# Matmuls that add zero, put into TensorE's stream after each tile's scores and PV

## The chip, the cores and the metric

One core of a Trainium2 chip (trn2). The metric is the device time of one execution in microseconds (us). Before the change: 1116.29 us, the median of 3 runs (1116.23 to 1120.81).

## The reference

Two attention blocks over 2048 tokens with 32 heads of 16 columns; their outputs stand side by side.

```python
def _B_ref(x, wqkv, wo):                       # problem "b": plain attention
    qkv = (x @ wqkv) ...                       # q, k, v: 32 heads x 2048 x 16
    scores = jnp.einsum('bhqd,bhkd->bhqk', q, k) * Dh ** (-0.5)
    o = jnp.einsum('bhqk,bhkd->bhqd', _softmax(scores), v)
    return o... @ wo
def _A_ref(x, wq, wk, wv, wo, beta):           # problem "a": 4 segments of 512 tokens
    for s in range(N):                         # causal attention inside the segment
        a_dot = _softmax(qs @ ks * scale + mask) @ vs
        a_mem = (phi(qs) @ M) / (phi(qs) @ z + 1e-06)     # memory of earlier segments
        o = g * a_mem + (1.0 - g) * a_dot
        M = M + phi(ks).T @ vs;  z = z + phi(ks).sum()
    ...
```

## The kernel before

Everything hangs on the exponentials of the scores. The kernel deals the scores out in 848 tiles, of 3 and 2 banks in turn (1536 and 1024 columns; a bank stands for 512 columns in PSUM here). For each tile TensorE (PE) computes up to three 32-row score matmuls at once (in the timelines below three take 0.61 us together at half clock), ScalarE (ACT) takes the exponential into `pT`, and two tiles later TensorE multiplies it with V (PV) into the accumulator `acc`. Some scores go to VectorE (DVE) instead, through `v_ps` and `vx`. Projections and other small work ("chores") are put between the tiles.

```python
BANKS = (3, 2); LAG = 2; VSHARE = 0.95
...
mp = ps_a = ms.enter_context(tc.tile_pool(name="ps_a", bufs=3, space=PSUM))  # acc, v_ps and chores
...
def scores(t):
    pt = last_s[0] = ps_s.tile([P, BANKS[t % 2], 512], F32, name="s_ps", tag=f"s{t % 2}")
    ...                                       # 32-row matmuls, one to a bank
    pin(nc.scalar.activation(pT[:, 0:n, :], pt[:, 0:n, :], ACT.Exp, scale=SCALE))
...
for t in range(NT):                           # program order of every engine
    now[0] = t
    run_until(t)                              # chores that are due
    scores(t)
    did = pv(t - LAG, 2)                      # up to two groups of 4 PV matmuls
    ...
    for _ in range((0 if did else 1) + ...):
        step_chore()                          # a matmul or so of a chore
    vfill((0.08 + 0.427 * len(tiles[t][0])) * VSHARE - ...)   # VectorE's pieces
```

The score tiles have two buffers. TensorE can write tile t+1 only when ScalarE has finished tile t-1 (its score matmuls wait 134.9 us for that in before), and should be done before ScalarE finishes tile t.

Of the kernel before, what the change touches and what calls it, by code (L numbers as in the profile page):

```python
# [13 lines left out]
BF16 = mybir.dt.bfloat16  # L14
# [5 lines left out]
P = 128  # L20
# [5 lines left out]
W = 512  # L26
# [8 lines left out]
XSCALE = SCALE * 1.4426950408889634 * 1024  # L35

C0, C1, C3 = 0.4580543, 0.4656991, 0.0762947
VSHARE = 0.95
VQUADS = 2
BANKS = (3, 2)  # L40
# [5 lines left out]
def kernel(  # L46
# [13 lines left out]
    nc = tc.nc  # L60
# [7 lines left out]
    def pin(ins):  # L68
        return tc.keep_in_program_order(ins)

    def mm(*a, **k):
        return pin(nc.tensor.matmul(*a, **k))  # L72
# [42 lines left out]
    def masks_gates():  # L115
        pin(nc.gpsimd.memset(bd[:], 0.0))
        for j in range(4):
            q = slice(32 * j, 32 * j + 32)
            for e in range(2):
                pin(nc.gpsimd.tensor_scalar(bd[q, e, q], bd[q, e, q], par[q, e:e + 1], None, ALU.add))  # L120
        pin(nc.scalar.activation(gcol[:], beta_t[:], ACT.Exp, scale=-1.0))
        pin(nc.vector.tensor_scalar(gcol[:], gcol[:], 1.0, None, ALU.add))
        pin(nc.vector.reciprocal(gcol[:], gcol[:]))
        pin(nc.vector.tensor_scalar(omg[:], gcol[:], -1.0, 1.0, ALU.mult, ALU.add))
        gv = gcol[:].rearrange("p (rt e) -> p rt e", e=2)
        pin(nc.vector.tensor_scalar(grow[:], gv[:, :, 0], par[:, 0:1], None, ALU.mult))
        pin(nc.vector.scalar_tensor_tensor(grow[:], gv[:, :, 1], par[:, 1:2], grow[:], ALU.mult, ALU.add))
# [192 lines left out]
    with ExitStack() as ms:  # L320
        big = ms.enter_context(tc.tile_pool(name="big", bufs=1))
        wk = ms.enter_context(tc.tile_pool(name="wk", bufs=1))
# [37 lines left out]
        for name, ch, rt in order:  # L360
            us = [dict(name=name, ch=ch, rt=rt, e=e, id=len(units) + e) for e in range(2)]
# [29 lines left out]
        first_tile, tiles = {}, []  # L391
# [102 lines left out]
        def bq_chores(ch, rt):  # L494
            qB[ch, rt] = wk.tile([P, 2, W], BF16, name="qB", tag=f"qB{rt}")
            key = ("b", ch, rt)
            chore(min(first_tile[key], first_tile.get(("v", ch, rt), NT)), do_q(mp, wk, wB, xTB[ch], rt, qB[ch, rt]))
# [16 lines left out]
        def flush():  # L514
            todo, held[0] = held[0], []
            for us, f in todo:
                credit[0] -= us
                f()

        current, now = [None], [0]  # L520

        def step_chore(new=True):

            flush()
            if current[0] is None:
                i = next((i for i, c in enumerate(chores) if c[4] <= now[0]), None)
                if not new or i is None:
                    return False
                current[0] = chores.pop(i)
            try:  # L530
                next(current[0][2])
                current[0][3] = max(1, current[0][3] - 1)
            except StopIteration:
                current[0] = None
                return step_chore(new)
            return True

        def run_until(t):
            while (current[0] is not None and current[0][0] <= t) or (chores and chores[0][0] <= t):
                step_chore()  # L540
# [6 lines left out]
        for rt in range(NRT):  # L547
            bq_chores(0, rt)
        okm = wk.tile([P, 2], F32, name="okm")
        last_s, cur = [None], [0]  # L550
        pvq = []
        accs, OT = {}, {}
# [45 lines left out]
        def vpiece(wq):  # L598

            w = wq[0]  # L600
            credit[0] -= w[1]
            w[1:] = next(w[0], None), True
            if w[1] is None:
                wq.popleft()
# [4 lines left out]
        def vfill(us):  # L609
            credit[0] = min(credit[0] + us, 1.4)  # L610
            while vfin or vwork:
                wq = vfin or vwork
                if wq is vwork and live[0] == 3 and not wq[0][2]:
                    return
                if credit[0] - sum(us for us, _ in held[0]) < 0.5 * wq[0][1]:
                    return
                vpiece(wq)
# [49 lines left out]
        def unit_done(u):  # L667
            name, ch, rt, e = u["name"], u["ch"], u["rt"], u["e"]
            st = fin[(name, ch, rt)]
            if e == 0:  # L670
                vdrain(vfin)
            fin_unit(wk, st, accs.pop(u["id"])[:], e)
            if u["id"] >= 62:
                flush()
                fin_half(wk, st, e)
                if e == 0:
                    sums_ok(wk, 0, 63, okm[:, 0:1])
                return
            if e == 0:
                return  # L680
            if (name, ch) not in OT:
                OT[(name, ch)] = wk.tile([P, NRT, W], BF16, name=f"OT_{name}", tag="OT", bufs=3)
            ot = OT[(name, ch)]
            while name == "a" and ch and ("mem", ch, rt) not in seen:
                step_chore()
            flush()

            def finish():
                yield from fin_pair(wk, st, name, rt, u["id"] - 1, ot[:, rt, :])
                i = order.index((name, ch, rt))  # L690
                if rt == NRT - 1:
                    due = first_tile[order[i + 1]] + 50 if i + 1 < len(order) else 10 ** 6
                    for sb in range(4):
                        chore(due, do_out(mp, wk, name, ot, woA if name == "a" else woB, ch, sb), 5)
            vpush(vfin, finish())
            if name == "a" and ch < NSEG - 1:
                mem_chores(ch, rt)
                seg_chores(ch + 1, rt)
            if name == "b" and ch < NSEG - 1:
                bq_chores(ch + 1, rt)  # L700

        def pv(t, lim):

            if cur[0] == len(units):
                return False
            u = units[cur[0]]
            ready = [q for q in pvq if q["u"] is u and q["t"] <= t and len(q["parts"]) == 4]
            if not ready or (lim == 2 and len(ready) < 2 and quads_left[u["id"]] > len(ready)):
                return False
            for q in ready[0:lim]:  # L710
                pvq.remove(q)
                live[0] -= "v" in q
                if u["id"] not in accs:
                    accs[u["id"]] = ps_a.tile([P, W], F32, name="acc", tag="misc")
                first = ("acc", u["id"]) not in seen
                seen.add(("acc", u["id"]))
                quads_left[u["id"]] -= 1
                v = vA[u["ch"]] if u["name"] == "a" else VB
                for pT, sl, j, (_, kb, col, w, c0) in q["parts"]:
                    h = 8 * u["rt"] + 2 * j + u["e"]  # L720
                    mm(accs[u["id"]][32 * j:32 * j + 32, c0:c0 + w], v[:, kb, VW * h:VW * h + 32],
                       pT[:, sl, col:col + w], start=first, stop=(quads_left[u["id"]] == 0),
                       tile_position=(0, 32 * j), skip_group_check=True)
            if quads_left[u["id"]] == 0:
                cur[0] += 1
                unit_done(u)
            return True

        for t in range(NT):
            now[0] = t  # L730
            run_until(t)
            scores(t)
            if t == 6:
                masks_gates()
            did = pv(t - LAG, 2)

            rate, n = 0.0, current[0][3] if current[0] else 0
            for c in chores:
                n += c[3]
                rate = max(rate, n / max(1, c[0] - t))  # L740
            for _ in range((0 if did else 1) + (rate > 0.55) + (rate > 1.1) + (rate > 1.8)):
                step_chore()
            vfill((0.08 + 0.427 * len(tiles[t][0])) * VSHARE - (0.69 if tiles[t][1] else 0.0))
            flush()
        vdrain(vfin)
# [15 lines left out]
        while len(pvq) > 1:  # L761
            assert pv(NT, 1)
        last = ps_s.tile([P, BANKS[NT % 2], 512], F32, name="l_ps", tag=f"s{NT % 2}")
        partial(0, last[:, 0, :])
        assert pv(NT, 1)
        partial(1, last[:, 1, :])
        tN = fin[("b", NSEG - 1, NRT - 1)]["tN"]
        for sb in range(4):
# [3 lines left out]
               skip_group_check=True)  # L772
# [157 lines left out]
```

## Time and profile before

| | before |
|---|---|
| time, median | 1116.29 us |
| ScalarE busy | 1005.5 us, 90% |
| TensorE mean granted clock | 0.632 |
| first to last exponential (trace) | 1084.7 us |
| floor of the 848 exponentials (trace) | 424 x (1331 + 904) ns = 948 us |

The granted clock is the share of full rate at which TensorE was let run; the clock records show only 1.0 and 0.5, and the mean stands in the table. Each stretch at one clock, but for the last, lasts a whole number of steps of 3.41 us (in before 1 to 45 of them). The floor is worked out from the 10th percentile of start-to-start times: 1331 ns after a 1536-column tile and 904 ns after a 1024-column one, counted from the trace. What the tiles take over it is called "lost" below: about 137 us.

From the page of before: busy time by engine, then busy tenths in 40 slices of the span, and the granted clock in tenths.

```profile
span 1118.5 us, 15007 instructions
...
PE 903.0 (81%) x5690; PEld 197.8 (18%) x5753; DVE 798.7 (71%) x1143; ACT 1005.5 (90%) x877; POOL 216.4 (19%) x361
...
PE   6898888797888787887898798787777887777775
...
ACT  3799999897889989999899879999999999999994
...
PEclk9989955555558866566555757555565576555556
```

ScalarE is nearly full; TensorE has half its clock in most slices after the fifth.

The groups of ScalarE by shape (busy us, mean ns of one, idle before it, what ended most of that idle time):

```profile
L635 ACT ACTIVATE pT<-s_ps 128x1536 bf16<-128x1536 f32 x424 | 619.2, 1460 | 70.7 <-PE s_ps L72 57.3 <-PE v_ps L72 7.8 <-ACT pT L635 0.6
L635 ACT ACTIVATE pT<-s_ps 128x1024 bf16<-128x1024 f32 x424 | 437.7, 1032 | 23.8 <-PE v_ps L72 11.6 <-PE s_ps L72 7.5 <-POOL pT L654 1.4
```

Idle before exponentials: 70.7 + 23.8 = 94.5 us.

Three stretches of before. The columns are the stretch, its length, busy us and number of instructions of PE, PEld, DVE, ACT and POOL, then the granted clock, the DMA share and GB/s:

```profile
40.00:150.00 110.00, 94.44 (x718) 26.75 (x722) 80.51 (x128) 103.51 (x92) 39.72 (x73) 0.93 0.04 10
150.00:700.00 550.00, 456.83 (x2808) 99.80 (x2842) 410.90 (x590) 494.88 (x433) 123.57 (x181) 0.60 0.03 9
700.00:1080.00 380.00, 304.01 (x1915) 59.22 (x1923) 280.17 (x379) 368.60 (x319) 33.73 (x58) 0.56 0.01 4
```

### The profile page before, as it was taken

The page shows a single profiled execution, that of the slowest core. Times are in us where ns is not written, and L with a number is a line of the kernel's source. Part 1 is how long each engine was busy: PE and PEld are TensorE (multiplying, and loading weights), DVE is VectorE, ACT ScalarE, POOL GpSimd, SP SyncE. Part 2 cuts the span into 40 slices and gives each one's busy share as a digit, 9 for nine tenths or more (in the row PEclk, how much of TensorE's full clock was granted, in tenths as well). Part 3 has the DMA queues.
Part 4 walks back from the last instruction along what each step waited for, and adds up shares of the span by engine and source line. Part 5 has one row for each costly group of instructions (what it writes and reads, how often), then busy time and mean ns, then how long its engine had stood idle before and what let it go on. Part 6 is the DMA issues. An engine that isn't in the chain of part 4 may idle for free.

```text
span 1118.5 us, 15007 instructions
## 1 busy us (share of the span) xinstructions
PE 903.0 (81%) x5690; PEld 197.8 (18%) x5753; DVE 798.7 (71%) x1143; ACT 1005.5 (90%) x877; POOL 216.4 (19%) x361
## 2 busy tenths in 40 slices
PE   6898888797888787887898798787777887777775
PEld 1222211111112211121111112111111121111111
DVE  2667877774778877779776867878577777876752
ACT  3799999897889989999899879999999999999994
POOL 3722310403213022141402304212020300000000
PEclk9989955555558866566555757555565576555556
DMA  7300000001000000000000000000000000000000
GB/s 183 81 6 20 6 1 5 1 1 23 6 1 4 31 11 5 1 20 10 1 4 2 19 20 6 6 1 1 1 1 1 1 29 10 1 1 1 1 1 23
DMA packets 34578, 15.23 MB, mean 14 GB/s; under 512 B 26304, under 2 KB 34496, under 8 KB 34496
## 3 DMA queue, kind: packets, MB, share of 16 engines
q1 hardware_dynamic: 32768, 12.47, 4.7%
q10 hardware_dynamic: 1728, 1.70, 0.5%
q8 instruction: 47, 0.77, 0.3%
q14 instruction: 35, 0.29, 0.1%
HBM read 4.20 MB, written 4.19 MB: 8 GB/s over the span
## 4 chain that ended last, share of the span: by engine, by line
ACT 39%; PE 33%; issue 12%; DVE 9%; POOL 5%; DMA 1%; SPq 0%; ACTq 0%; DVEq 0%; POOLq 0%
ACT pT L635 38%; PE s_ps L72 13%; PE acc L72 9%; PE v_ps L72 3%; DVE vv L572 3%; POOL pT L654 3%; PE k_ps L72 2%; PE q_ps L72 2%; PE o_ps L72 2%; DVE vv L569 1%; DVE vx L643 1%; ACT ex L182 1%; POOL qA L174 1%; DMA xT_a<-in_A_x_dram 1%; POOL po L184 1%
## 5 line engine op out<-in xcount | busy, mean ns | idle before, releaser
L635 ACT ACTIVATE pT<-s_ps 128x1536 bf16<-128x1536 f32 x848 | 993.2, 1246 | 94.5 <-PE s_ps L72 64.8
L72 PE MATMUL s_ps<-qB,KB 32*128 32x512 bf16 x1800 | 408.5, 555 | 136.3 <-ACT pT L635 123.2
L643 DVE TENSOR_SCALAR vx<-v_ps 128x512 uint16<-128x512 f32 x248 | 169.7, 684 | 124.0 <-PE v_ps L72 120.4
L72 PE MATMUL acc<-pT,VB 128*32 128x512 bf16 x1800 | 223.3, 576 | 5.2 <-DVE vx L643 4.8
L72 PEld LDWEIGHTS <-KB 32*128 32x128 bf16 x2048 | 86.6, 98 | 509.4 <-issue 506.1
L654 POOL TENSOR_SCALAR_AFFINE_SELECT pT<-pT 128x256 bf16<-128x256 bf16 (+2 forms) x242 | 108.7, 478 | 317.2 <-ACT pT L635 316.4
L72 PE MATMUL v_ps<-qB,KB 32*128 32x512 bf16 x248 | 137.1, 553 | 7.0 <-DVE aT L250 3.9
L243 DVE STREAM_TRANSPOSE tT<-acc 128x512 f32<-128x512 f32 x64 | 45.6, 712 | 66.0 <-PE acc L72 65.5
L569 DVE TENSOR_SCALAR vv<-vv 128x2048 f16<-128x2048 f16 x124 | 86.6, 698 | 2.0
L572 DVE TENSOR_TENSOR vv<-vx 128x2048 f16<-128x2048 f16 x62 | 77.5, 1250 | 1.3
L72 PE MATMUL s_ps<-qA,kA 32*128 32x384 bf16 (+3 forms) x512 | 66.0, 364 | 15.4 <-ACT pT L635 11.7
L572 DVE TENSOR_TENSOR vv<-vv,vi 128x2048 uint16<-128x2048 uint16 x62 | 76.2, 1230 | 1.3
L572 DVE TENSOR_TENSOR vv<-vv,vx 128x2048 f16<-128x2048 f16 x62 | 76.1, 1228 | 1.3
L174 POOL TENSOR_SCALAR qB<-qc,par 128x512 bf16<-128x512 bf16 x32 | 32.9, 1038 | 203.8 <-DVE qc L171 203.8
L72 PEld LDWEIGHTS <-VB 128*32 128x32 bf16 x2048 | 36.0, 105 | 117.5 <-issue 117.4
L174 POOL TENSOR_SCALAR qA<-qc,par 128x512 bf16<-128x512 bf16 x32 | 25.7, 815 | 127.8 <-DVE qc L171 127.7
L72 PE MATMUL acc<-pT,vA 128*32 128x128 bf16 (+3 forms) x512 | 43.5, 371 | 6.6 <-POOL pT L654 6.1
L569 DVE TENSOR_SCALAR vx<-vx 128x2048 uint16<-128x2048 uint16 x62 | 44.7, 721 | 1.5
L569 DVE TENSOR_SCALAR vi<-vx 128x2048 uint16<-128x2048 uint16 x62 | 43.1, 695 | 1.0
L72 PE MATMUL acc<-vv,VB 128*32 128x512 bf16 x248 | 36.8, 582 | 2.9 <-DVE vv L572 2.4
L171 DVE CAST qc<-q_ps 128x512 bf16<-128x512 f32 x32 | 22.0, 687 | 19.8 <-PE q_ps L72 15.2
L72 PE MATMUL k_ps<-xT_a,w_a 128*128 128x512 bf16 x58 | 26.6, 499 | 10.2 <-DMA xT_a<-in_A_x_dram 9.5
(151 smaller groups left out, 536.6 us busy)
## 6 DMA issues: line engine op xcount, KB each, us to landing
out_dram<-osb SPq DMA_DIRECT2D x31, 128.0 KB, 1.7
w_b<-in_B_wqkv_dram SPq DMA_DIRECT2D x3, 512.0 KB, 4.9
phk<-phkT SPq DMA_TRANSPOSE x48, 2.3
w_a<-in_A_wk_dram ACTq DMA_DIRECT2D x1, 512.0 KB, 4.1
w_a<-in_A_wq_dram ACTq DMA_DIRECT2D x1, 512.0 KB, 5.8
w_a<-in_A_wv_dram ACTq DMA_DIRECT2D x1, 512.0 KB, 8.1
wo_a<-in_A_wo_dram SPq DMA_DIRECT2D x1, 512.0 KB, 4.5
wo_b<-in_B_wo_dram SPq DMA_DIRECT2D x1, 512.0 KB, 5.4
```

The source lines that it names most:

```text
L72: return pin(nc.tensor.matmul(*a, **k))
L171: vlater(0.69, lambda: pin(nc.vector.tensor_copy(qc[:], ps[:])))
L174: pin(nc.gpsimd.tensor_scalar(dst[:, e, :], qc[:], par[:, e:e + 1], 0.0, ALU.mult, ALU.add))
L182: pin(nc.scalar.activation(ex[:], src, ACT.Exp))
L184: pin(nc.gpsimd.tensor_scalar(po[:], src, 0.0, None, ALU.max))
L243: vlater(0.72, lambda: pin(nc.vector.transpose(st["tT"][:, e].rearrange("p c d -> p (c d)"), acc)))
L569: pin(nc.vector.tensor_scalar(o, i, s1, s2, op0, op1))
L572: pin(nc.vector.tensor_tensor(o, i0, i1, op=op))
L635: pin(nc.scalar.activation(pT[:, 0:n, :], pt[:, 0:n, :], ACT.Exp, scale=SCALE))
L643: pin(nc.vector.tensor_scalar(x[0][:, vb[0], :], vt[:], XSCALE, 32768.0, ALU.mult, ALU.add))
L654: pin(nc.gpsimd.affine_select(out=blk, in_=blk, compare_op=ALU.is_ge, fill=0.0, base=0, pattern=[[0, len(sls)], [1, P]], channel_multiplie ...
```

## The change

The intent: TensorE's granted clock seems to follow its activity (counted in the trace of before, it fell after steps in which something streamed for 0.42 of the time or less, and rose after steps with 0.70 or more), so give it activity. The change keeps an account of TensorE's work per tile, in us at full clock. Where it falls behind 0.72 of the time of ScalarE's tile, 128x128 matmuls with zero weights and zero data are put into the stream. They add zero to the accumulator that is open, so they need no PSUM buffer of their own and alter no result.

```diff
+PESHARE = 0.72
...
+        work = [0.0]
...
                 next(current[0][2])                    # a step of a chore
+                work[0] += 0.17
...
+        zeros = wk.tile([P, W], BF16, name="zeros")
+        nc.gpsimd.memset(zeros[:], 0.0)
+        def idle_work(us):
+            work[0] = max(work[0] - us * PESHARE, -1.0)
+            acc = accs.get(cur[0])
+            while acc is not None and work[0] < -0.11:
+                mm(acc[:], zeros[:, 0:P], zeros[:], start=False, stop=False, skip_group_check=True)
+                work[0] += 0.22
...
                 pvq.remove(q)                          # in pv(): a group of 4 PV matmuls
+                work[0] += 0.27
...
             scores(t)
...
+            work[0] += 0.28
             did = pv(t - LAG, 2)
...                                                     # chores
+            idle_work(0.1 + 0.427 * len(tiles[t][0]))
             vfill(...)
```

## The prediction

> **What bounds the kernel now.** ScalarE: the page's engine table has it 90% busy (1005.5 of 1118.5 us), 993 us of it on the 848 exponentials of score tiles. In the trace, back-to-back exponentials start 1331 ns apart after a 1536-column tile, 904 ns after a 1024-column one (10th percentiles), so 424 pairs need at least 948 us. First to last takes 1085 us: 137 us are lost between. The group view puts idle time before them at 94.5 us, 64.8 of it on s_ps and 19 on v_ps.
>
> TensorE's mean granted clock is 0.632; after 150 us it is mostly 0.5. A 512-column matmul follows its like after 216 ns at full clock, 427 at half; scores to PV takes 315 against 533. So at half clock the next scores are often late. Excess over the floor by phase and clock: 150 to 700 us, half clock 71 us on 324 tiles (50 of it in gaps under 1 us), full clock 16 us on 91 (4 under 1 us); after 700 us, half clock 28 us on 295 tiles, full clock 0.2 us on 37. The 21 gaps over 1 us (e.g. 5.9 us at 268) are mostly chains through DVE and POOL, at either clock.
>
> **What grants the clock.** It changes on a grid of 3.41 us. By my count of streaming time per step, half goes to full only after steps over about 75-80% occupied, full to half only after steps under about 45%. [...]
>
> **What the change adds.** After each tile it tops TensorE's work up to 0.72 x (0.1 + 0.427 x banks) us: 713 us over 848 tiles. Own work in the author's units: scores 237, 640 PV quads 173, about 690 chore steps 118. Remainder 185 us: at most 840 fillers, I expect 650 to 850 (none where no accumulator is open). Nothing is removed or moved. At full clock 72% is well over the 45% that holds it; at half clock the same work fills TensorE, so it comes back within one or two steps.
>
> **Cost.** A filler streams 216 ns, plus about 100 ns for changing weights (315 against 216). With that, TensorE takes 1.9 to 2.1 us of a pair's 2.235: fillers fit, but some scores will be late, above all where chores are dense and after unit ends, when up to four fillers come at once. I allow 12 us.
>
> **Sum.** Small gaps at half clock after 150 us: 50 + 27 = 77 us. At the full-clock rate about 14 remain, so 62 to gain; 90% coverage gives 56; less 12 for late scores: 44 us. Start-up and long chains stay. 1116 - 44 = 1072.
>
> **Prediction:** 1071 us, range 1048 to 1097. Faster by over 2% 0.79, within 2% 0.16, slower 0.05.
>
> **Right or wrong.** Right if the mean clock rises above 0.88, ScalarE's idle time on s_ps falls from 65 to under 35 us and its busy share goes to 93-95%; after 700 us tiles should be on the floor. The 4 to 6 us gaps near 195 and 268 should stay. Wrong if the clock stays at half (fillers of zeros don't count as activity), if waits of scores behind fillers exceed the gain, or if DVE (71% busy) becomes the limit, seen as longer waits of v_ps on vx.

The limits named are the author's count in the trace of before. Recounted in it, with streaming as in the table under "Fillers of 32 rows", the 20 steps before a rise were streaming for 0.70 to 0.93 of the time and the 21 before a fall for 0 to 0.42. The 100 ns for changing weights are the author's estimate, the difference of 315 and 216 ns in that trace; that a change of weights costs this was not shown (see point 2 below).

## More of the kernel before

The steady part of the program at half clock (start us, length us, engine, instruction, in brackets the idle time before it):

```profile
781.03 0.61 PE L72 MATMUL s_ps<-qB,KB 32*128 32x512 bf16 x3 [1.18 <-ACT pT L635]
...
781.57 1.04 PE L72 MATMUL acc<-pT,VB 128*32 128x512 bf16 x8
...
782.54 0.61 PE L72 MATMUL s_ps<-qB,KB 32*128 32x512 bf16 x2
...
783.28 0.61 PE L72 MATMUL s_ps<-qB,KB 32*128 32x512 bf16 x3
...
784.33 0.61 PE L72 MATMUL s_ps<-qB,KB 32*128 32x512 bf16 x2 [0.43 <-ACT pT L635]
...
785.67 0.61 PE L72 MATMUL s_ps<-qB,KB 32*128 32x512 bf16 x3 [0.73 <-ACT pT L635]
```

In this stretch TensorE needs 0.54 us from the scores to PV and 0.97 us for PV: it is busy, at half speed, and idle only where it waits for ScalarE to free a score tile. (Some 60 matmul records of this trace are missing: 5690 matmuls stand beside 5753 weight loads.)

## The result, and the profile after

The time is 1083.78 us, median of 4 runs (1079.11 to 1084.76); before, with the run that was added beside it, 1118.03 (1116.23 to 1120.81, 4 runs). The ratio is 0.9683, 95% interval 0.9646 to 0.9721: 3.2% faster. Ratios here are the mean time of one kernel's fast runs over that of the other's of the same rounds, so not quite the ratio of the medians.

From the page of after, the same lines:

```profile
span 1082.3 us, 16757 instructions
...
PE 910.6 (84%) x6596; PEld 262.5 (24%) x6596; DVE 797.5 (74%) x1143; ACT 985.4 (91%) x877; POOL 214.7 (20%) x362
...
PE   5998879886888988888898879888888898888885
...
ACT  2799989897979899989999979999999999999994
...
PEclk9999965899789899989899889999999999999998
```

The granted clock is 0.931 on average. TensorE's busy share went from 81% to 84% only, though 843 matmuls were added: the others got shorter (a 512-column score matmul of block b took 555 ns in the mean before, 400 after). The busy share alone doesn't tell how near TensorE is to its limit here: 81% at a clock of 0.632 was more of a limit than 84% at 0.931.

The groups of ScalarE by shape, after:

```profile
L647 ACT ACTIVATE pT<-s_ps 128x1536 bf16<-128x1536 f32 x424 | 654.3, 1543 | 57.9 <-PE s_ps L73 50.1 <-PE v_ps L73 5.7 <-POOL pT L666 0.8
L647 ACT ACTIVATE pT<-s_ps 128x1024 bf16<-128x1024 f32 x424 | 473.5, 1117 | 22.5 <-PE v_ps L73 11.0 <-PE s_ps L73 7.4 <-POOL pT L666 1.7
```

Each exponential now seems longer (1543 ns against 1460). It isn't slower: it starts earlier, during the one before. Counted from the trace, consecutive exponentials overlap by 153 us in sum, before by 64. The trace of before shows an overlap of some 120 ns where nothing waits: a lone exponential takes about 1452 ns (1536 columns) or 1025 ns (1024), and the next starts after 1331 or 904. The profile page counts overlapped time once, so both its busy time (993.2 to 974.9 us for all 848) and its idle time (94.5 to 80.4) fell; 18.3 + 14.1 = 32.4 us is nearly the whole gain, and over half of it never showed as idle time.

The same place in the program as before, at full clock, with fillers (`acc<-zeros`):

```profile
780.91 0.39 PE L73 MATMUL s_ps<-qB,KB 32*128 32x512 bf16 x3
...
781.23 0.40 PE L73 MATMUL acc<-pT,VB 128*32 128x512 bf16 x4
781.46 0.39 PE L73 MATMUL acc<-vv,VB 128*32 128x512 bf16 x4
...
781.83 0.39 PE L73 MATMUL s_ps<-qB,KB 32*128 32x512 bf16 x2
...
782.15 0.60 PE L73 MATMUL acc<-zeros 128*128 128x512 bf16 x2
...
783.17 0.40 PE L73 MATMUL s_ps<-qB,KB 32*128 32x512 bf16 x3 [0.41 <-ACT pT L647]
...
783.50 0.82 PE L73 MATMUL acc<-zeros 128*128 128x512 bf16 x3
...
784.25 0.39 PE L73 MATMUL s_ps<-qB,KB 32*128 32x512 bf16 x2
```

Scores now come every 0.92 to 1.34 us, as ScalarE takes them, and fillers fill most of what is left.

The three stretches, after:

```profile
40.00:150.00 110.00, 94.87 (x728) 26.70 (x725) 80.10 (x126) 102.40 (x92) 40.63 (x76) 0.95 0.05 12
150.00:700.00 550.00, 460.99 (x3284) 128.65 (x3281) 424.04 (x610) 500.07 (x447) 124.75 (x182) 0.89 0.04 9
700.00:1080.00 380.00, 327.87 (x2448) 99.46 (x2447) 280.17 (x386) 366.92 (x326) 30.45 (x56) 0.99 0.02 5
```

The last stretch has the clock at 0.99 (0.56 before, without the matmuls of zeros); the middle one at 0.89 (0.60). What the tiles lost over the floor, counted from both traces (tile 100 starts at 150 us before and 152 after, tile 525 at 714 and 700 us; a gap here is start-to-start time over the floor; long means over 1 us; gaps under 30 ns are left out):

| lost, us | before | after |
|---|---|---|
| tiles 100 to 524, gaps under 1 us | 54 | 30 |
| tiles 100 to 524, long gaps | 33.0 | 41.6 |
| from tile 525, all gaps | 25 | 5 |

The late part came down to within 5 us of its floor. The middle part gave back 8.6 us of the 24 it gained, as longer long gaps. A long gap after the change, in the middle part:

```profile
605.56 0.61 PE L73 MATMUL s_ps<-qA,kA 32*128 32x256 bf16 x6 [0.73 <-ACT pT L647]
...
606.10 0.94 PE L73 MATMUL acc<-pT,vA 128*32 128x512 bf16 x8
...
606.97 1.89 PE L73 MATMUL acc<-zeros 128*128 128x512 bf16 x4
...
608.79 0.55 PE L73 MATMUL s_ps<-qA,kA 32*128 32x384 bf16 x4
...
609.44 1.02 ACT L647 ACTIVATE pT<-s_ps 128x1024 bf16<-128x1024 f32 x1 [1.68 <-POOL pT L666]
```

An accumulator has just been opened, the account stands at its lowest, the clock is at half from 602.3 to 609.1 us, after a step with streaming for only 0.39 of the time: four fillers come at once, take 1.82 us to the start of the next scores, and ScalarE waits for those; the gap here is 1.8 us by the count from the trace. (The bracket in the last line names another waiter, POOL, by the profile's last semaphore; ScalarE's scores began at 608.79.)

### The profile page after: what moved, and what is told of

It reads as the page before. It is cut to its first block, busy times and chain, and to the rows that moved or that the text cites. A ratio compares the mean times of both kernels' runs of the same rounds, so it can differ in the third digit from the quotient of the medians.

```text
span 1082.3 us, 16757 instructions
## 1 busy us (share of the span) xinstructions
PE 910.6 (84%) x6596; PEld 262.5 (24%) x6596; DVE 797.5 (74%) x1143; ACT 985.4 (91%) x877; POOL 214.7 (20%) x362
## 4 chain that ended last, share of the span: by engine, by line
ACT 45%; PE 23%; issue 15%; DVE 11%; POOL 4%; DMA 1%; SPq 0%; ACTq 0%; DVEq 0%; POOLq 0%
ACT pT L647 44%; PE acc L73 8%; PE s_ps L73 7%; DVE vv L584 4%; PE v_ps L73 3%; PE k_ps L73 2%; POOL pT L666 2%; DVE vx L655 2%; PE q_ps L73 2%; DVE vv L581 1%; PE o_ps L73 1%; ACT ex L183 1%; POOL qA L175 1%; DMA xT_a<-in_A_x_dram 1%; DVE tT L244 1%
## 5 line engine op out<-in xcount | busy, mean ns | idle before, releaser
L647 ACT ACTIVATE pT<-s_ps 128x1536 bf16<-128x1536 f32 x848 | 974.9, 1330 | 80.4 <-PE s_ps L73 57.5
L73 PE MATMUL s_ps<-qB,KB 32*128 32x512 bf16 x1800 | 296.9, 400 | 96.3 <-ACT pT L647 88.3
L73 PE MATMUL acc<-zeros 128*128 128x512 bf16 x843 | 270.4, 394 | 0.0
L73 PEld LDWEIGHTS <-KB 32*128 32x128 bf16 x2048 | 100.2, 91 | 371.9 <-issue 364.0
L73 PE MATMUL acc<-pT,VB 128*32 128x512 bf16 x1800 | 153.0, 406 | 6.5 <-DVE vx L655 6.4
L73 PE MATMUL v_ps<-qB,KB 32*128 32x512 bf16 x248 | 100.0, 403 | 7.6 <-DVE aT L251 4.7
L73 PEld LDWEIGHTS <-zeros 128*128 128x128 bf16 x843 | 67.3, 99 | 119.9 <-issue 98.7
L73 PE MATMUL s_ps<-qA,kA 32*128 32x384 bf16 (+3 forms) x512 | 59.2, 331 | 12.8 <-ACT pT L647 11.0
L73 PE MATMUL acc<-pT,vA 128*32 128x128 bf16 (+3 forms) x512 | 38.2, 327 | 3.3 <-POOL pT L666 2.6
L73 PEld LDWEIGHTS <-kA 32*128 32x128 bf16 x512 | 17.4, 94 | 78.0 <-issue 74.8
```

Source lines behind the costliest of these rows:

```text
L73: return pin(nc.tensor.matmul(*a, **k))
```

## The experiments

Theory: the gain comes from the granted clock, which is taken to follow TensorE's activity; the fillers themselves only cost. Rivals: the added instructions change the order or the pace in which TensorE dispatches (no clock needed); or the clock counts, but what measures activity is something other than the time in which anything streams. For what was missing from the middle part: fillers in the way of scores, against chains through VectorE and POOL. All kernels gave correct results. Labels of one batch shared a chip and its runs of before: the experiments up to the fillers of 32 rows were one batch, those from the share of 0.60 to the cap a second, VectorE's share with the first cap and floor a third, and the last two runs a fourth.

### Fillers of one column

```diff
-mm(acc[:], zeros[:, 0:P], zeros[:], ...)
+mm(acc[:, 0:1], zeros[:, 0:P], zeros[:, 0:1], ...)
```

> The same fillers at the same places, but of one column: the instructions stay, the streaming time goes. Clock theory (the gain comes from the granted clock, which follows the share of time that TensorE streams): clock 0.60 to 0.66, time 1114 to 1124 us, no better than before. Rival, order theory (the extra instructions change when scores and PV are dispatched, whatever the clock): time near 1084 us at a low clock.

Measured: 1126.19 us (1123.17 to 1128.39), ratio 1.0091 (1.0040 to 1.0142), clock 0.615. The time is just above the stated range. The order theory falls: with every instruction in place and no streaming, nothing is gained. It also prices the instructions themselves, each with its weight load: some 9 us for 843 (1126.19 against 1117.11), mostly at half clock.

### Fillers only late, only early

```diff
-while acc is not None and work[0] < -0.11:
+while now[0] >= 525 and acc is not None and work[0] < -0.11:     # e2; e3: now[0] < 525
```

> Fillers only from tile 525 on (after about 700 us). By my count of lost time per tile the last 323 tiles gave 21 of the 35 us. Clock theory: 1095 to 1099 us, clock about 0.6 before 700 us and about 0.98 after. If the gain of the late part needed the early part (phases shifted against each other), it would be under 15 us, over 1103 us.

> Fillers only up to tile 524. Expected gain 14 us: 1102 to 1106 us; clock about 0.9 from 190 to 700 us and about 0.56 after. The gains of this run and of the one with late fillers should add up to that of the change, within 4 us.

Measured: late 1095.48 us, ratio 0.9822 (0.9754 to 0.9890), clock 0.98 from 700 us on; early 1102.77 us, ratio 0.9875 (0.9824 to 0.9926), clock 0.89 from 150 to 700 us. The gains, 1.8% and 1.25%, add up to 3.0%, against 3.2% for the change. Both runs are in their ranges. (By the 2% rule for verdicts alone, late is unclear and early is the same; both intervals lie below 1.) The late 323 tiles, two fifths of all, give more than half of the gain; in before, only one of the 16 gaps over 1 us after 150 us lay there.

### Fillers of 32 rows

```diff
-mm(acc[:], zeros[:, 0:P], zeros[:], ...)
+mm(acc[:], zeros[0:32, 0:P], zeros[0:32, :], ..., tile_position=(0, 0), ...)
```

> Fillers of 32 rows instead of 128 in the same places, streaming as long over a quarter of the array. If the gate follows the time in which anything streams: clock 0.91 to 0.95 and 1080 to 1088 us as in the change. If it follows the occupied area of the array: late in the program the area share with such fillers is about 0.45, so the clock falls to 0.65 to 0.8 and the time is 1095 to 1112 us.

(The gate is whatever sets the granted clock. The area share of 0.45 is the author's estimate; counted in the trace of after, matmuls fill 0.58 of the array from 700 to 1065 us, and 0.37 with each filler put at a quarter.)

Measured: 1254.44 us (1244.53 to 1261.60), ratio 1.1212 (1.1143 to 1.1281), clock 0.607. Neither range holds; the direction is the second theory's, and it is far worse than either. From the page of this kernel:

```profile
span 1259.9 us, 16757 instructions
...
PE 1174.9 (93%) x6596; PEld 273.7 (22%) x6596; DVE 801.5 (64%) x1143; ACT 1024.3 (81%) x877; POOL 209.1 (17%) x362
...
ACT  4889896777779797887788679888888799888884
```

and two stretches of it (the granted clock is the third number from the right):

```profile
150.00:700.00 550.00, 517.91 (x2807) 106.27 (x2805) 360.32 (x518) 444.03 (x383) 106.11 (x161) 0.56 0.03 7
700.00:1080.00 380.00, 366.43 (x2050) 88.62 (x2047) 250.96 (x345) 319.21 (x271) 43.78 (x77) 0.59 0.02 6
```

TensorE is busy for 93% of the span and the clock stays mostly at half (0.607 on average). The trace shows six steps of the clock's grid in which something streamed all the time (share 1.0) and which were still followed by half clock; in those the occupied area of the array, rows x columns, was 0.33 to 0.45. So in those steps streaming time alone did not bring the clock up. Here is the count of area in five traces (a matmul's rows x columns over 128 x 128, the largest form in the traces, while it streams, per step of 3.41 us; streaming is counted from the recorded start, 216 ns at full clock or 427 at half for 512 columns; another choice of its start moves single figures by up to 0.05):

| kernel | full to half: largest area | stayed full: smallest area | half to full: smallest area | stayed half: largest area | stayed half: largest share of time |
|---|---|---|---|---|---|
| before | 0.36 | 0.25 | 0.61 | 0.76 | 0.86 |
| after | 0.38 | 0.32 | 0.69 | 0.77 | 0.84 |
| one column | 0.37 | 0.38 | 0.73 | 0.76 | 0.85 |
| 32 rows | 0.37 | 0.31 | 0.71 | 0.77 | 1.00 |
| share 0.60 | 0.37 | 0.36 | 0.71 | 0.78 | 0.86 |

The columns overlap, so area is the better measure here and not an exact rule. Over the thirteen traces with clock records, one limit for the way up (an area of 0.76) misplaces 80 of 1609 steps; no limit on time does better than to say that the clock never comes up, which misplaces 272. For the way down the two fit about alike: a limit of 0.37 on area misplaces 45 of 2637 steps, one of 0.43 on time 37. A streaming share of 0.70 to 1.00 came with the way up in the other four kernels of the table, whose matmuls together filled 0.61 of the array or more in those steps. Of the two forms tried, only the whole-array filler brought the clock up (0.931 against 0.607). (Whether rows alone or rows x columns count, these runs don't tell: only rows were varied.)

This run also shows what fillers cost when they don't pay: at half clock they stream for some 427 ns each (in its trace two in a row take 1.06 us at 1005 us, one 0.63 at 1002), and 137 us are lost (1254 against 1117). Not all of that is the clock: these fillers lie on 32 rows that scores use as well, and in this trace 428 of the 2048 score matmuls of block b start with no other of them within 30 ns, against 45 in after, so many scores no longer run up to three at once.

### Fewer and more fillers

```diff
-PESHARE = 0.72          # 843 fillers
+PESHARE = 0.60          # e5: 303 fillers;  e6: 0.90, 1602 fillers
```

> Share 0.60 instead of 0.72: 303 fillers instead of 843. Waits in which a filler stood longest in TensorE's way before a late score sum to 18 us in the change's trace. If those are what was mis-sized, and the clock holds (occupied area at full clock about 0.47 a step, over the 0.38 at which it fell), the time is 1074 to 1081 us. If the clock no longer holds through the thin steps, it is 0.75 to 0.88 and the time 1086 to 1098 us.

> Share 0.90: 1602 fillers. Clock 0.94 to 0.97. The clock can give no more, so what is added is cost: [...] scores come late everywhere, 1110 to 1170 us. If fillers fit for nothing in idle time, the time stays at 1080 to 1086 us.

(In the first of these 0.47 is the author's estimate; 0.38 is the largest area before a fall in the trace of after. From the second a clause is cut that set a cost for each change of weights, which no trace shows; that scores would come late everywhere rested on it.)

Measured: with 0.60, 1101.78 us, ratio 0.9856 (0.9818 to 0.9894), clock 0.776: 0.63 from 150 to 700 us, 0.93 after. That is the second case, some 4 us over its range. From tile 525 on, 13 us are lost over the floor (before 25, after 5), so the late part keeps 12 of its 20 us with few fillers; the middle part's gaps under 1 us are back at 56 us, since chores of other kinds are booked as work and the account then asks for no filler before 528 us.

With 0.90, 1119.94 us, ratio 1.0028 (0.9989 to 1.0068), clock 0.972: in the stated range, and all of the gain is gone at the highest clock of all. From its page and its TensorE groups:

```profile
PE 1024.7 (92%) x7355; PEld 295.9 (26%) x7355; DVE 796.6 (71%) x1143; ACT 1005.4 (90%) x877; POOL 211.5 (19%) x362
```

```profile
L73 PE MATMUL acc<-zeros 128*128 128x512 bf16 x1602 | 457.0, 388 | 0.0
L73 PE MATMUL s_ps<-qB,KB 32*128 32x512 bf16 x1800 | 284.8, 386 | 24.1 <-ACT pT L647 23.5
```

In that trace the gaps in which a filler stood longest in the way before the late scores sum to 65 us; in after's, to 18 us. So a filler is not free at full clock either. Of the three shares tried 0.72 is the best; nothing between them was tried.

### Fillers half as long

```diff
-mm(acc[:], zeros[:, 0:P], zeros[:], ...);            work[0] += 0.22;  threshold -0.11
+mm(acc[:, 0:256], zeros[:, 0:P], zeros[:, 0:256], ...); work[0] += 0.11;  threshold -0.055
```

> Fillers of 256 columns, twice as many (1686), the same streaming time. If late scores come from the grain of a filler (one that has just begun when ScalarE frees the bank), the late-score waits fall by some 5 us: 1076 to 1081 us. If they come from the sum of the work or from bursts, no change: 1081 to 1088 us. Clock 0.92 to 0.94 either way.

Measured: 1086.47 us, ratio 0.9727 (0.9692 to 0.9761), clock 0.920: no gain over the change (0.9683 in another batch). So no sign that the grain of one filler makes scores late. It is not excluded: this kernel has 843 instructions more, and what they cost (some 9 us for as many one-column fillers, at half clock) could hide the 5 us that were expected.

### A cap on work booked in advance

```diff
-work[0] = max(work[0] - us * PESHARE, -1.0)
+work[0] = min(max(work[0] - us * PESHARE, -1.0), 0.5)
```

> The account of work done is capped at 0.5 us in advance, so the dense chores of the start no longer forbid fillers until 187 us; 894 fillers. The stretch at half clock from 145 to 189 us (44 us) should go. In that stretch tiles 100 to 150 lose 13.2 us over the floor, 7 of them in chains that the clock doesn't touch: gain 3 to 5 us, 1078 to 1082 us, clock 0.95 to 0.97. If the stretch is bound by chains through DVE and POOL alone, no gain.

Measured: 1079.86 us (1078.84 to 1081.53), ratio 0.9666 (0.9633 to 0.9700), clock 0.941. In after no filler is sent until 187 us, since the chores of the start are booked as work done; the clock is at half from 145 to 189 us. With the cap it is 0.96 in those 44 us, and tiles 100 to 149 lose 10.0 us over the floor instead of 13.2. The time is in the range, the clock just under its own (0.95 to 0.97); the gain over the change is small, and this batch didn't hold the change itself.

### VectorE's share

```diff
-VSHARE = 0.95
+VSHARE = 0.88
```

> The change, with VSHARE 0.88 instead of 0.95: DVE's exponential pieces are dealt out more thinly, so the copies that free a buffer for TensorE stand behind fewer of them. If the long waits between 150 and 700 us (19 gaps over 1 us, 41.6 us, in 29.7 of them TensorE idle) come from copies behind DVE's pieces, these fall by 6 to 12 us: 1072 to 1079 us. If they are chains that VSHARE doesn't order (POOL, transposes), no change: 1080 to 1087 us; if DVE's quads then come too late for their units, slower.

Measured: 1265.30 us, ratio 1.1313 (1.1260 to 1.1367), clock 0.833. The hope was wrong and the last case came, slower, by far more than I had thought of. Who waited for whom, longest first (engine, line, what for, us, times, longest), in this kernel and in after:

```profile
ACT pT L647 <- PE s_ps L73: 176.6, 121, 12.0
...
PE acc L73 <- DVE vv L584: 79.7, 29, 5.4
```

```profile
ACT pT L647 <- PE s_ps L73: 57.5, 52, 12.2
...
PE acc L73 <- DVE vv L584: 3.1, 3, 1.4
```

PV takes its groups unit by unit, so a group that VectorE has not finished stops TensorE, and the scores behind it: 79.7 us of such waits against 3.1. A VSHARE of 0.88 is too slow for this order. The experiment therefore doesn't tell whether the stalls in the middle part come from copies behind VectorE's pieces; that stays open.

### Cap and floor

```diff
-work[0] = max(work[0] - us * PESHARE, -1.0)
+work[0] = min(max(work[0] - us * PESHARE, -0.35), 0.5)
```

> The account of work capped at 0.5 us in advance (as in the run before) and at 0.35 us of arrears instead of 1.0, so at most two or three fillers come at once after a unit's end. Bursts of 3 to 5 fillers at half clock cost 1.0 to 1.8 us each in five gaps of the change's trace, 7 us together. If bursts are what cost, 1073 to 1078 us. If a burst is what brings the clock back, its loss shows: the clock falls below 0.92 and the time is 1081 to 1090 us.

Measured: four fast runs, 1068.59 to 1077.46 us (median of the four about 1076), ratio 0.9615 (0.9563 to 0.9668), clock 0.940 to 0.952. One of the five executions, the profiled one, took 2229.79 us. In its trace the step from scores to PV takes 832 ns (315 at full clock, 533 at half), fillers follow each other after 587 to 840 ns (216 at full clock, 427 at half), TensorE is 96% busy, and the profile has no record of a granted clock at all. It is set aside.

> The kernel of the run before once more (same instructions), for a profile of a fast run and to see whether the one execution of 2229 us comes again. Fast runs at 1072 to 1080 us, clock 0.94 to 0.955; in the trace the gaps over 1 us with a filler longest in the way fall from 6 us to under 3 us and those with TensorE idle stay near 30 us. If the slow execution belongs to this kernel, it shows in at least one of these six; if it was a state of the chip, in none.

> The changed kernel itself, beside the version with cap and floor on the same chip: 1080 to 1087 us, 5 to 10 us over it. If the two are within 3 us, cap and floor are not shown to be worth anything.

Measured on one chip: cap and floor 1080.02 us (1076.00 to 1082.81, 5 runs), ratio 0.9663 (0.9637 to 0.9689); the change itself 1084.92 us (1082.95 to 1087.78, 5 runs), ratio 0.9711 (0.9689 to 0.9734). The clock of cap and floor was 0.930 to 0.942, in part just under its range. The medians are 4.9 us apart; it was just under what was expected, and the two intervals touch. In the trace of cap and floor, long gaps between tiles 100 and 524 sum to 34.1 us (41.6 in after, 42.3 in its repetition), those with a filler longest in the way to 2.8 us (6.0 and 9.1), those with TensorE idle to 26.6 us (29.7 and 28.3).

So in the trace most of the bursts are gone from the long gaps. That it is the floor that removes them, and not the cap, shows in the trace of the cap alone: by a recount that puts about 1.2 us more under fillers, long gaps with a filler longest in the way sum to 7.3 us in after, 10.4 in its repetition, 10.2 with the cap alone and 3.9 with both. In time, the floor is not shown to add anything: the cap alone stood at 0.9666 (0.9633 to 0.9700), cap and floor at 0.9615 and 0.9663, on three chips, and the floor alone was not run. The slow execution did not come again in five; with one in ten executions of this kernel, and none of any other, that does not clear the kernel.

## Why the prediction was right or wrong

The time: predicted 1071 us, range 1048 to 1097, measured 1083.78. In the range, and faster by over 2% as forecast; the gain is 34 us where 44 were predicted.

1. **What bounds it and what would move it: right.** The gain follows the clock (one column: nothing gained; late and early fillers: each gains where its clock is up), the clock went to 0.931 (predicted over 0.88), 843 fillers (predicted 650 to 850), it came back within one or two steps in 11 of the 13 stretches at half clock between 199 and 653 us, and after 700 us the tiles stand 5 us in all over the floor.
2. **Small gaps, "62 to gain; 90% coverage gives 56; less 12 for late scores: 44 us": right in sum.** Gaps under 1 us after 150 us, those under 30 ns included, went from 80.7 to 37.8 us: 42.9 us gained. Gaps with a filler longest in the way sum to 18 us, 6 of them in long gaps, so the 12 us allowed among the small ones fit. That fit has some luck in it: "about 100 ns for changing weights", an estimate, was the wrong reason. In the trace of after, one filler follows another at full clock after 216 to 228 ns though each has its own weight load (843 fillers, 843 loads); the 312 to 323 ns stand between a score matmul and a filler, whichever comes first.
3. **"Start-up and long chains stay": wrong, and this is where most of the missing 10 us lie.** The two gaps named, near 195 and 268 us, did stay (4.3 and 5.9 us before, 4.3 and 6.3 after). But all gaps over 1 us after 150 us grew from 34.2 to 41.6 us. Of the 8.6 us that the middle part's grew, 6.0 are gaps with a filler longest in the way, and 4.5 are longer times with TensorE idle, less 2.0 elsewhere. I had allowed for bursts, but as late scores among the small gaps; at half clock, where they run at 0.43 us a filler (0.40 to 0.43 in the trace), they make long ones. With the floor at 0.35 us most of them are gone from the trace again, and the other traces agree: long gaps in the middle sum to 29 to 33 us in the four kernels with few or no full-length fillers there (before, one column, late only, share 0.60) and to 39 to 44 in the five with the change's fillers there (after, its repetition, early only, half as long, cap). The place of the loss is shown; that removing it gains time beyond the cap is not.
4. **The rule for the clock's way up, over about 75-80% of streaming time: wrong in its measure.** Occupied area tells it better in these traces (80 of 1609 steps misplaced, against 272). The forecast came out all the same, because the change's fillers are 128x128; with 32-row fillers the same rule would have forecast 1080 to 1088 us, and 1254 was measured. What was right is that the falls go with a share and not with one long gap, and its limit of about 45% of time still fits the way down about as well as area does (37 of 2637 steps misplaced at 0.43 of time, 45 at 0.37 of area): in before, 14 of the 21 falls came after a step whose longest idle time was 0.52 to 0.95 us, at an area of at most 0.36.
5. **Two of the signs named were badly chosen.** ScalarE's idle time on s_ps fell from 64.8 to 57.5 us only (predicted under 35), and its busy share rose to 91% (predicted 93 to 95). About 20 us of that idle time is start-up in both, and most of the rest is the long gaps; the gain lies in overlap of exponentials, which the page counts as less busy time. Start-to-start times against their floor are the sign to use.

The sum, from first to last exponential: 42.9 gained in small gaps after 150 us, 7.4 given back in long ones, about 1.0 lost before 150 us: 34.5, against 34.8 measured (1084.7 to 1049.9). What remains open is the cause of the long gaps with TensorE idle in the middle part (29.7 us in after), which stood between 23 and 30 us by the recount in every trace, with fillers or without, but for the two much slower kernels (32 rows, VSHARE 0.88).

## What to carry to other kernels

TensorE was kept at speed by work that has no use, because it waited anyway (134.9 us for ScalarE in before) and its clock rose with the added work (0.632 to 0.931). What work did this was found by runs: here whole-array matmuls of 512 columns (0.931) and not 32-row ones (0.607) or those of one column (0.615). Its price must be read where the clock is not up yet. Put in about as little as holds the clock (0.72 of the time here; 0.60 and 0.90 were worse), and limit the credits and debts of the account: a burst can come while the clock is at half, as at 607 us in after, and then costs double (427 ns a filler against 216). Small portions, and the limit on debts by itself, were not shown to gain time here. When producer and consumer are pipelined, measure start-to-start times against their floor: idle time and mean durations hide lost overlap.
